# Bucket-masked attention and a routed expert layer: query tiles in groups of three in place of two

## The chip, the cores and the metric

The kernel runs on one NeuronCore of a Trainium2 chip. The metric is the device time of one execution in microseconds (us). The core has five engines that run side by side, each with its own queue: TensorE (PE; its weight loads are listed apart, as PEld), VectorE (DVE), ScalarE (ACT), GpSimd (POOL) and SyncE (SP), which here only issues DMA transfers. Semaphores order them against each other.

## What is computed

The inputs are q, k and v of shape (4, 8, 768, 64) in float32: 4 batches, 8 heads, 768 tokens, 64 numbers each. The attention is dense, with a mask from hashed buckets:

```python
q_bits = (np.einsum('bhsd,dk->bhsk', q, proj) > 0).astype(np.int64)
k_bits = (np.einsum('bhsd,dk->bhsk', k, proj) > 0).astype(np.int64)
...
mask = q_bucket[:, :, :, None] == k_bucket[:, :, None, :]
scores = scale * np.matmul(q, k.transpose(0, 1, 3, 2))
scores = np.where(mask, scores, -1000000000.0)
...
attn = attn / (np.sum(attn, axis=-1, keepdims=True) + 1e-09)
return np.matmul(attn, v).astype(np.float32)
```

The result, as 3072 tokens of 512 numbers, goes through an expert layer: each token is sent to the expert of its largest gate logit (one of 8), passes w1 (512 x 1024), a ReLU and w2 (1024 x 512) of that expert, and is scaled by two gates.

## The kernel before, in words

**Attention.** The 32 heads are worked off as 16 pairs (index g). A pair has 12 *steps*, so the attention has NSTEP = 192. One step is one tile of 128 queries of one head against all 768 keys. The first six steps of a pair (half hf = 0) cover the first 384 queries of its two heads, the last six the other 384. What happens to the tile of step s:

- `scores(s)`: four matmuls (L457; K = 128 and K = 76, each over two halves of the keys) into a PSUM tile `ps_s`, of which there are two. DVE then writes the masked scores to the SBUF tile `sc` and takes their minimum `mn` (L461). There are LAG + 2 tiles `sc`.
- `soft(s)`: ACT takes the exponential in place, and its row sum into one column of `rsum` (L469).
- `normal(s0)`: once for a group of steps. DVE adds 1e-9 to the group's row sums and takes the reciprocal (L476, L477); POOL multiplies each `sc` of the group by it (L479).
- `transposed(s)`: PE turns `sc` in six blocks of 128 x 128 (L490), three each into one of two PSUM tiles `ps_t`; ACT copies these to `pts` in SBUF, two copies of 128 x 384 (L491).
- `weighted(hb, c)`: a *pair of weighted sums*, one matmul for each of the two heads (L501): the values of key block c times `pts` of the half hb, added up in PSUM `ps_a` over c = 0 to 5. After the sixth pair DVE copies the sum to `ot` (L504).

**The order of the work.** PE, DVE, ACT and POOL run in the order in which the code is written; SP's transfers are placed by the framework's scheduler. The loop below writes the steps in groups of GROUP, here 2. In a group, each step writes its scores, then the transposition of the tile LAG steps back, then its exponential, then the small work that `plan` has put down for that step. At the start of a group `normal` handles the group before. At the end of a group come the pairs of weighted sums that the table `products` lists for its steps, one for each step.

```python
for s0 in range(0, NSTEP + LAG, GROUP):
    for s in range(s0, s0 + GROUP):
        if s < NSTEP:
            live[s] = scores(s)
        if s == s0 and 0 <= s - GROUP < NSTEP:
            normal(s - GROUP)
        if 0 <= s - LAG < NSTEP:
            transposed(s - LAG, live.pop(s - LAG))
        if s < NSTEP:
            live[s] = soft(s, *live[s])
        for fn in at.get(s, ()):
            fn()
    for s in range(s0, s0 + GROUP):
        for fn in products.get(s, ()):
            fn()
```

With GROUP = 2, LAG is 2 * GROUP = 4. `plan` places the preparation of the next pair of heads: `load` (queries and keys by DMA), `project` (bucket signs, L365), `split_hi` (POOL, L408) and `split_lo` (DVE, L416), which cut the operands into a high and a low part, `spread` (SBUF-to-SBUF DMAs that put the parts where the matmuls need them), and `load_v` (the pair's values `vt`, of which there are two buffers; L357). It also places `rows` (a DVE transpose, L513, and four DMAs to `x_dram`) and the routing of each finished batch (`logits`, L535, and others).

**Expert layer.** After the attention, the chosen expert's weights are streamed in and the tokens gathered; the change does not touch this part.

Of the kernel before, what the change touches and what calls it, by code (L numbers as in the profile page):

```python
# [19 lines left out]
B, H, S, D = 4, 8, 768, 64  # L20
# [19 lines left out]
TURN_DOWN = ((None, 0), (2, None), (None, 1), (3, None), (None, 2), (None, 3))  # L40
NROUND = (NTOK - min(CAPS) + CAP0 - 1) // CAP0
NCC = DM // P
GROUP = 2
NFB = F // P
MASKED = 1.0e9
PEN = float(2.0 ** 31)
# [10 lines left out]
def lsh_attention_then_moe(  # L57
# [26 lines left out]
    for h, s in ((0, 1.0), (1, -1.0)):  # L84
        hs = slice(h * D, (h + 1) * D)
        c = 2 * NB * h
# [239 lines left out]
    with ExitStack() as actx:  # L326
# [11 lines left out]
        at, products = {}, {}  # L338


        LAG = 2 * GROUP

        def plan(step, *fns):
            at.setdefault(step, []).extend(fns)


        def load(g, heads=(0, 1)):
            st = pairs[g]
            st.setdefault("qk", [])
            for j in heads:  # L350
                t = hp.tile([P, S], F32, name="qk", bufs=2)
                nc.sync.dma_start(t, qkT[2 * g + j])
                st["qk"].append(t)

        def load_v(g):
            pairs[g]["v"] = tp.tile([P, 2, NT, D], F32, name="vt", bufs=2)
            nc.sync.dma_start(pairs[g]["v"], v[g])  # L357

        def project(g, heads=(0, 1)):
            st = pairs[g]  # L360
            pp = ps_m.tile([P, HS], F32, name="ps_m")
            for j in heads:
                for n in range(2):
                    r = 32 * (2 * j + n)
                    nc.tensor.matmul(pp[r:r + 32], pjc[:, 0:32], st["qk"][j][:, n * HS:(n + 1) * HS],  # L365
                                     start=True, stop=True)
            bt = hp.tile([P, HS], F32R, name="bt", bufs=2)
            hs = slice(heads[0] * D, (heads[-1] + 1) * D)
            nc.vector.tensor_scalar(bt[hs], pp[hs], thr[hs], scl[hs], ALU.is_gt, ALU.mult)
            st["bt"] = bt  # L370
            for k in ("xl", "yl", "xr", "yr"):
                st.setdefault(k, [None, None])

        def first_head():

# [28 lines left out]

        def split_hi(g, j):
            st = pairs[g]
            xl = hp.tile([P, S], F32R, name="xl")
            nc.gpsimd.tensor_scalar(xl, st["qk"][j], sgn, 0.0, ALU.mult, ALU.add)  # L408
            st["xl"][j] = xl

        def split_lo(g, j, n):
            st = pairs[g]
            if n == 0:
                st["yl"][j] = hp.tile([P, S], F32R, name="yl")
            cs = slice(n * HS, (n + 1) * HS)
            nc.vector.scalar_tensor_tensor(st["yl"][j][:, cs], st["qk"][j][:, cs], sgn, f32(st["xl"][j][:, cs]),  # L416
                                           ALU.mult, ALU.subtract)

        def spread(g, j, hurry=False):
            st = pairs[g]  # L420
            xl, yl, bt = f32(st["xl"][j]), f32(st["yl"][j]), f32(st["bt"])
            st["xr"][j] = hp.tile([P, S], F32R, name="xr")
            st["yr"][j] = hp.tile([D + 2 * NB, S], F32R, name="yr")
            xr, yr = f32(st["xr"][j]), f32(st["yr"][j])
            if hurry:
                qk = st["qk"][j]
                for t in ("xr", "yr"):
                    nc.scalar.copy(st[t][j][0:D], qk[D:P])
                nc.gpsimd.tensor_scalar(st["xr"][j][D:P], yl[D:P], 1.0, 0.0, ALU.mult, ALU.add)
                nc.scalar.activation(st["xl"][j][D:P], qk[0:D], AF.Copy, scale=-0.125)  # L430
            else:
                nc.sync.dma_start(xr[0:D], xl[D:P])
                nc.sync.dma_start(yr[0:D], xl[D:P])
                nc.sync.dma_start(xr[D:P], yl[D:P])
                nc.sync.dma_start(xl[D:P], xl[0:D])
            for n in range(2):
                r = 32 * (2 * j + n)
                cs = slice(n * HS, (n + 1) * HS)
                nc.sync.dma_start(yr[D:D + 2 * NB, cs], bt[r + 2 * NB:r + 4 * NB])
                nc.sync.dma_start(yl[D:D + 2 * NB, cs], bt[r:r + 2 * NB])  # L440
# [8 lines left out]
        def scores(s):  # L449
# [5 lines left out]
            for l, r, k, first in ((st["xl"][j], st["xr"][j], P, True), (st["yl"][j], st["yr"][j], kb, False)):  # L455
                for n in range(2):
                    nc.tensor.matmul(ss[:, n, 0:HS], l[0:k, qs], r[0:k, n * HS:(n + 1) * HS],  # L457
                                     start=first, stop=not first)
            sc = tp.tile([P, 2, HS], F32, name="sc", bufs=LAG + 2)
            mn = sp.tile([P, 1], F32, name="mn")  # L460
# [3 lines left out]
        def soft(s, sc, mn):  # L464
            if s % GROUP == 0:
                sums[s // GROUP] = sp.tile([P, GROUP], F32, name="rsum")
            pr = sc.rearrange("p a b -> p (a b)")
            k = s % GROUP
            nc.scalar.activation(pr, pr, AF.Exp, bias=mn, scale=-1.0,  # L469
                                 accum_out=sums[s // GROUP][:, k:k + 1])  # L470
            return pr

        def normal(s0):

            rs = sums.pop(s0 // GROUP)
            nc.vector.tensor_scalar(rs, rs, 1e-9, None, ALU.add)  # L476
# [16 lines left out]
        def weighted(hb, c):  # L493
            g, hf = hb // 2, hb % 2
            st = pairs[g]
            if c == 0:
                st["av"] = ps_a.tile([P, HS], F32, name="ps_a")
            if c == NT - 1 and hf == 0:
                st["ot"] = gp.tile([P, S], F32, name="ot", bufs=4)
            for j in range(2):  # L500
                nc.tensor.matmul(st["av"][j * D:(j + 1) * D], st["v"][:, j, c], blocks[hb][j][:, c],  # L501
                                 start=(c == 0), stop=(c == NT - 1))
            if c == NT - 1:
                nc.vector.tensor_copy(st["ot"][:, hf * HS:(hf + 1) * HS], st["av"])  # L504

        def rows(g, hf, whole=True):

            b, i = divmod(g, H // 2)
            st = pairs[g]
            if hf == 0:  # L510
                st["xb"] = gp.tile([P, S // 32, 32], F32, name="xb", bufs=2)
            ts = slice(hf * HS // 32, (hf + 1) * HS // 32)
            nc.vector.transpose(st["xb"][:, ts].rearrange("p n c -> p (n c)"), st["ot"][:, hf * HS:(hf + 1) * HS])  # L513
            if whole:
                if hf == 0:
                    return
                ts = slice(0, S // 32)
            xv = x_dram[b * S:(b + 1) * S].rearrange("(n r) c -> r n c", r=32)
            for a in range(4):
                nc.sync.dma_start(xv[:, ts, i * P + 32 * a:i * P + 32 * (a + 1)], st["xb"][32 * a:32 * (a + 1), ts])  # L520
# [110 lines left out]
        for g in range(NP):  # L631
            s0 = 12 * (g - 1)
            if g >= 2:
                plan(s0 - 5, lambda g=g: load(g))
            if g >= 1:
                s0 += 2 * (g == 1)
                plan(s0 + 1, lambda g=g: project(g))
                plan(s0 + 5, lambda g=g: load_v(g))
                for j in range(2):
                    plan(s0 + 1 + 2 * j, lambda g=g, j=j: split_hi(g, j))  # L640
                    for n in range(2):
                        plan(s0 + 3 + 2 * j + n, lambda g=g, j=j, n=n: split_lo(g, j, n))
                    plan(s0 + 4 + 2 * j, lambda g=g, j=j: spread(g, j))
            for hf in range(2 if g + 1 < NP else 1):
                for c in range(NT):
                    products.setdefault(12 * g + 6 * hf + 6 + LAG + c, []).append(lambda hb=2 * g + hf, c=c: weighted(hb, c))
                if g + 1 < NP:
                    plan(12 * g + 6 * hf + 13 + LAG, lambda g=g, hf=hf: rows(g, hf))
        for b in range(B - 1):
            r = routing(b)  # L650
            for n, fn in ((11, lambda r=r: r["logits"](0, H // 2)), (12, lambda r=r: r["logits"](1, H // 2)),
                          (14, lambda r=r: r["tokens"](0, H // 2)), (16, lambda r=r: r["tokens"](1, H // 2)),
                          (18, r["best"]), (19, r["choose"]), (20, r["gates"]),
                          (22, r["prefix"]), (22, r["ranks"]), (23, r["cols"]), (24, r["hot"]), (26, r["table"]), (26, r["entries"])):
                plan(12 * (H // 2) * (b + 1) + n, fn)

        r = routing(B - 1)
        s0 = 12 * (NP - 1)
# [91 lines left out]
        with tc.manual_schedule(engines=MANUAL):  # L750
# [12 lines left out]
            live = {}  # L763
# [9 lines that stand above are left out]
# [58 lines left out]
    with tc.manual_schedule(engines=MANUAL):  # L831
# [16 lines left out]
        for r in range(E):  # L848
            n = CAPS[r] if r else CAP0
# [167 lines left out]
```

## Time and profile before

| what | value |
|---|---|
| median of 3 runs | 825.32 us (824.72 to 827.4) |
| profiled execution, its own time | 825.83 us |
| span of the profiled execution | 824.0 us |
| PE busy, share of the span | 779.8 us, 95% |
| DVE, ACT, POOL busy | 529.9, 460.9, 359.9 us |
| mean granted TensorE clock | 0.985 |

The span runs from the first to the last instruction of the program; the time of the execution is 1.8 us longer. In rows of the timeline the columns are start and duration in us, engine, line, operation, tiles, shapes and count; in square brackets stands how long the engine had been idle before, and what released it. PE's rows are pipelined, so starts of the weight loads (PEld) tell more of PE's pace than the lengths of its rows. A weighted-sum matmul and a transposition block have one or two records each: a pair of weighted sums shows as four records of L501, a transposition as six of L490.

### The profile page before, as it was taken

The page shows a single profiled execution, that of the slowest core. Times are in us where ns is not written, and L with a number is a line of the kernel's source. Part 1 is how long each engine was busy: PE and PEld are TensorE (multiplying, and loading weights), DVE is VectorE, ACT ScalarE, POOL GpSimd, SP SyncE. Part 2 cuts the span into 40 slices and gives each one's busy share as a digit, 9 for nine tenths or more (in the row PEclk, how much of TensorE's full clock was granted, in tenths as well). Part 3 has the DMA queues.
Part 4 walks back from the last instruction along what each step waited for, and adds up shares of the span by engine and source line. Part 5 has one row for each costly group of instructions (what it writes and reads, how often), then busy time and mean ns, then how long its engine had stood idle before and what let it go on. Part 6 is the DMA issues. An engine that isn't in the chain of part 4 may idle for free. (4 is left out here: it accounts for less than half of the span.)

```text
span 824.0 us, 13863 instructions
## 1 busy us (share of the span) xinstructions
PE 779.8 (95%) x4648; PEld 606.3 (74%) x4648; DVE 529.9 (64%) x1293; ACT 460.9 (56%) x934; POOL 359.9 (44%) x377
## 2 busy tenths in 40 slices
PE   6899999999999999999999998999999898979894
PEld 3667676677666666766767677888989897959693
DVE  5666666687656885765977562468586867575730
ACT  5767777677767777867777611442424242424240
POOL 5544445444544444544366843306171616160410
PEclk9999999999999999999999999999999999998998
DMA  3543654454455446445545323543545343535231
GB/s 120 135 101 90 140 123 90 117 136 103 108 132 133 82 113 149 92 106 135 132 104 143 85 71 116 179 133 113 169 131 168 131 155 121 160 121 170 89 101 36
DMA packets 84176, 99.54 MB, mean 121 GB/s; under 512 B 57183, under 2 KB 58671, under 8 KB 84096
## 3 DMA queue, kind: packets, MB, share of 16 engines
q1 hardware_dynamic: 79472, 84.66, 40.3%
q0 software_dynamic: 4480, 13.90, 4.9%
q8 instruction: 39, 0.64, 0.3%
q14 instruction: 41, 0.34, 0.1%
q10 hardware_dynamic: 144, 0.01, 0.0%
HBM read 60.07 MB, written 13.11 MB: 89 GB/s over the span
## 5 line engine op out<-in xcount | busy, mean ns | idle before, releaser
L479 POOL TENSOR_SCALAR sc<-sc,rsum 128x768 f32<-128x768 f32 x192 | 182.5, 963 | 224.6 <-DVE rsum L477 149.2
L461 DVE TENSOR_SCALAR_CACHE_REDUCE sc<-ps_s 128x768 f32<-128x768 f32 x192 | 183.2, 955 | 101.4 <-PE ps_s L457 95.6
L491 ACT COPY pts<-ps_t 128x384 f32<-128x384 f32 x384 | 164.3, 481 | 104.1 <-PE ps_t L490 103.6
L469 ACT ACTIVATE sc<-sc,mn 128x768 f32<-128x768 f32 x192 | 181.5, 945 | 12.7 <-DVE sc L461 11.5
L490 PE MATMUL ps_t<-ident,sc 128*128 128x128 f32 x1152 | 158.4, 273 | 1.5 <-POOL sc L479 0.7
L501 PE MATMUL ps_a<-pts,vt 128*64 128x384 f32 x768 | 145.9, 502 | 0.0
L490 PEld LDWEIGHTS ps_t<-ident,sc 128*128 128x128 f32 x1152 | 137.1, 140 | 11.6 <-POOL sc L479 3.0
L457 PE MATMUL ps_s<-xr,xl 128*128 128x384 f32 x384 | 117.9, 388 | 3.5 <-DMA xl<-xl 2.8
L270 PE MATMUL ps_s<-xh,w1h 128*128 128x256 f32 (+7 forms) x288 | 98.8, 343 | 8.7 <-POOL xh L254 4.9
L457 PEld LDWEIGHTS ps_s<-xr,xl 128*128 128x128 f32 x384 | 58.8, 193 | 63.3 <-issue 25.5
L270 PE MATMUL ps_s<-xlo,w1h 128*128 128x256 f32 (+7 forms) x288 | 96.9, 336 | 4.6 <-POOL xlo L255 4.3
L457 PE MATMUL ps_s<-yr,yl 76*128 76x384 f32 x384 | 100.7, 344 | 0.0
L270 PE MATMUL ps_s<-xh,w1l 128*128 128x256 f32 (+7 forms) x288 | 96.5, 335 | 1.6 <-DVE w1l L151 1.6
L250 DVE STREAM_TRANSPOSE xt<-xg 32x128 f32<-32x128 f32 x300 | 90.7, 302 | 5.7 <-POOL xlo L255 1.9
L287 POOL DMA_INDIRECT out_dram<-yo,sid x29 | 31.7, 1095 | 143.2 <-ACT yo L286 102.4
L501 PEld LDWEIGHTS ps_a<-pts,vt 128*64 128x64 f32 x768 | 46.9, 137 | 59.4 <-issue 54.5
L457 PEld LDWEIGHTS ps_s<-yr,yl 76*128 76x128 f32 x384 | 71.2, 192 | 0.2 <-DMA yl<-bt 0.2
L280 ACT ACTIVATE hh<-ps_s 128x256 fp32r<-128x256 f32 (+8 forms) x40 | 29.0, 726 | 70.2 <-PE ps_s L270 70.2
L281 DVE SCALAR_TENSOR_TENSOR hl<-ps_s,hh 128x256 fp32r<-128x256 f32 (+8 forms) x40 | 33.8, 848 | 50.2 <-ACT hh L280 49.6
L270 PEld LDWEIGHTS ps_s<-xh,w1h 128*128 128x128 f32 x288 | 55.0, 191 | 13.8 <-POOL xh L254 6.4
L150 ACT CAST w1h<-w_raw 128x1024 fp32r<-128x1024 f32 x28 | 28.8, 1046 | 64.5 <-DMA w_raw<-in_w_dram 64.4
L270 PEld LDWEIGHTS ps_s<-xlo,w1h 128*128 128x128 f32 x288 | 55.0, 191 | 7.3 <-POOL xlo L255 6.3
(185 smaller groups left out, 1061.8 us busy)
## 6 DMA issues: line engine op xcount, KB each, us to landing
w_raw<-in_w_dram SPq DMA_DIRECT2D x64, 512.0 KB
qk<-in_qkT_dram SPq DMA_DIRECT2D x32, 384.0 KB
vt<-in_v_dram SPq DMA_DIRECT2D x16, 384.0 KB
xr<-xl SPq DMA_DIRECT2D x30, 192.0 KB
yr<-xl SPq DMA_DIRECT2D x30, 192.0 KB
xr<-yl SPq DMA_DIRECT2D x30, 192.0 KB
xl<-xl SPq DMA_DIRECT2D x30, 192.0 KB
x_dram<-xb SPq DMA_DIRECT2D x60, 96.0 KB
```

The lines of the kernel that those rows point to most:

```text
L250: nc.vector.transpose(w[32 * a:32 * a + 32, :, q:q + 32], src[:, a])
L270: nc.tensor.matmul(ps, l, r, start=first and k == 0, stop=last and k == len(pairs) - 1)
L280: nc.scalar.activation(hh, ph, AF.Relu)
L281: return lambda: nc.vector.scalar_tensor_tensor(hl, ph, 0.0, f32(hh), ALU.max, ALU.subtract)
L287: nc.gpsimd.indirect_dma_start(out=out[:, :], out_offset=bass.IndirectOffsetOnAxis(ap=sid[0:n, r, a:a + 1], axis=0), in_=yo[0:n], in_offse ...
L457: nc.tensor.matmul(ss[:, n, 0:HS], l[0:k, qs], r[0:k, n * HS:(n + 1) * HS], start=first, stop=not first)
L461: nc.vector.tensor_scalar(sc, ss[:, :, 0:HS], MASKED, None, ALU.min, ALU.min, accum_out=mn)
L469: nc.scalar.activation(pr, pr, AF.Exp, bias=mn, scale=-1.0, accum_out=sums[s // GROUP][:, k:k + 1])
L479: nc.gpsimd.tensor_scalar(live[s0 + k], live[s0 + k], rs[:, k:k + 1], 0.0, ALU.mult, ALU.add)
L490: nc.tensor.transpose(tr[:, c], pr[:, (3 * h + c) * P:(3 * h + c + 1) * P], ident)
L491: nc.scalar.copy(pts[:, 3 * h:3 * h + 3, t * P:(t + 1) * P], tr)
L501: nc.tensor.matmul(st["av"][j * D:(j + 1) * D], st["v"][:, j, c], blocks[hb][j][:, c], start=(c == 0), stop=(c == NT - 1))
```

## The change

GROUP becomes 3, and LAG becomes GROUP + 1, which is 4 as before, so tiles and buffers keep their numbers. A group is now three steps, with three pairs of weighted sums at its end. The pairs of weighted sums are put down one step earlier (5 + LAG in place of 6 + LAG), `logits(0)` one step earlier (10 in place of 11), and `load_v` five steps later (10 in place of 5). Setting up the empty lists of a pair moves from `project` to `split_hi`, and does no work on the chip.

```diff
-GROUP = 2
+GROUP = 3
...
-        LAG = 2 * GROUP
+        LAG = GROUP + 1
...
-                plan(s0 + 5, lambda g=g: load_v(g))
+                plan(s0 + 10, lambda g=g: load_v(g))
...
-                    products.setdefault(12 * g + 6 * hf + 6 + LAG + c, []).append(lambda hb=2 * g + hf, c=c: weighted(hb, c))
+                    products.setdefault(12 * g + 6 * hf + 5 + LAG + c, []).append(lambda hb=2 * g + hf, c=c: weighted(hb, c))
...
-            for n, fn in ((11, lambda r=r: r["logits"](0, H // 2)), (12, lambda r=r: r["logits"](1, H // 2)),
+            for n, fn in ((10, lambda r=r: r["logits"](0, H // 2)), (12, lambda r=r: r["logits"](1, H // 2)),
```

**The order on PE, before,** in the group that starts at step 90. `ps_s` is the scores' tile, `sc` the tile that is transposed; the numbers tell tiles apart and have no relation between the two kernels. Four weighted sums follow.

```order
L457 MATMUL ps_s_2783<-xr_2402,xl_2308 128x384 x2
L457 MATMUL ps_s_2783<-yr_2403,yl_2365 128x384 x2
L490 MATMUL ps_t_2795<-ident_72,sc_2668 128x128 x3
L490 MATMUL ps_t_2800<-ident_72,sc_2668 128x128 x3
L457 MATMUL ps_s_2818<-xr_2467,xl_2367 128x384 x2
L457 MATMUL ps_s_2818<-yr_2468,yl_2435 128x384 x2
L490 MATMUL ps_t_2826<-ident_72,sc_2692 128x128 x3
L490 MATMUL ps_t_2831<-ident_72,sc_2692 128x128 x3
```

**The same place on PE with the change:** the group of steps 90, 91 and 92. Six weighted sums follow.

```order
L457 MATMUL ps_s_2737<-xr_2362,xl_2274 128x384 x2
L457 MATMUL ps_s_2737<-yr_2363,yl_2336 128x384 x2
L490 MATMUL ps_t_2750<-ident_72,sc_2624 128x128 x3
L490 MATMUL ps_t_2755<-ident_72,sc_2624 128x128 x3
L457 MATMUL ps_s_2773<-xr_2428,xl_2338 128x384 x2
L457 MATMUL ps_s_2773<-yr_2429,yl_2393 128x384 x2
L490 MATMUL ps_t_2781<-ident_72,sc_2651 128x128 x3
L490 MATMUL ps_t_2786<-ident_72,sc_2651 128x128 x3
L457 MATMUL ps_s_2796<-xr_2362,xl_2274 128x384 x2
L457 MATMUL ps_s_2796<-yr_2363,yl_2336 128x384 x2
L490 MATMUL ps_t_2804<-ident_72,sc_2680 128x128 x3
L490 MATMUL ps_t_2809<-ident_72,sc_2680 128x128 x3
```

A third step stands between two blocks of weighted sums; the tile transposed is that of four steps back in both.

**The multiplications on POOL and what they wait for on DVE, before.** POOL's rows, the tiles of steps 86 to 90:

```order
L479 TENSOR_SCALAR sc_2668<-sc_2668,rsum_2685 128x768
L479 TENSOR_SCALAR sc_2692<-sc_2692,rsum_2685 128x768
L479 TENSOR_SCALAR sc_2721<-sc_2721,rsum_2740 128x768
L479 TENSOR_SCALAR sc_2758<-sc_2758,rsum_2740 128x768
L479 TENSOR_SCALAR sc_2788<-sc_2788,rsum_2805 128x768
```

DVE's rows at step 90 (its minimum is the first row):

```order
L461 TENSOR_SCALAR sc_2788,mn_2789<-ps_s_2783 128x768
L476 TENSOR_SCALAR rsum_2740<-rsum_2740 128x2
L477 RECIPROCAL rsum_2740<-rsum_2740 128x2
L416 SCALAR_TENSOR_TENSOR yl_2776<-qk_2498,pj_64,xl_2708 128x384
L461 TENSOR_SCALAR sc_2823,mn_2824<-ps_s_2818 128x768
```

The tiles that PE transposes in this group, 2668 and 2692, are multiplied by `rsum_2685`, one group earlier than `rsum_2740`, whose reciprocal stands here.

**The same with the change.** POOL's rows, the tiles of steps 86 to 90:

```order
L479 TENSOR_SCALAR sc_2624<-sc_2624,rsum_2589 128x768
L408 TENSOR_SCALAR xl_2673<-qk_2459,pj_64 128x768
L479 TENSOR_SCALAR sc_2651<-sc_2651,rsum_2669 128x768
L479 TENSOR_SCALAR sc_2680<-sc_2680,rsum_2669 128x768
L479 TENSOR_SCALAR sc_2712<-sc_2712,rsum_2669 128x768
L479 TENSOR_SCALAR sc_2742<-sc_2742,rsum_2760 128x768
```

DVE's rows at step 90:

```order
L461 TENSOR_SCALAR sc_2742,mn_2743<-ps_s_2737 128x768
L476 TENSOR_SCALAR rsum_2669<-rsum_2669 128x3
L477 RECIPROCAL rsum_2669<-rsum_2669 128x3
L416 SCALAR_TENSOR_TENSOR yl_2728<-qk_2459,pj_64,xl_2673 128x384
L461 TENSOR_SCALAR sc_2778,mn_2779<-ps_s_2773 128x768
```

The tiles that PE transposes at the second and the third step of this group, 2651 and 2680, are now multiplied by `rsum_2669`, whose reciprocal stands in this same group, behind the minimum of its first step (`ps_s_2737`).

**The load of the values on SP,** before and then with the change:

```order
L434 DMA xr<-yl 64x768
L439 DMA yr<-bt 12x384
L357 DMA vt<-in_v_dram 128x768
L435 DMA xl<-xl 64x768
L440 DMA yl<-bt 12x384
```

```order
L440 DMA yl<-bt 12x384
L352 DMA qk<-in_qkT_dram 128x768 x2
L357 DMA vt<-in_v_dram 128x768
L520 DMA x_dram<-xb 32x24x32 x4
L432 DMA xr<-xl 64x768
```

It moves from the middle of a pair's spreading transfers to behind the loads of queries and keys.

More of the change, by code (lines that the diff above doesn't have):

```diff
@@ L370, in project @@
             st["bt"] = bt
-            for k in ("xl", "yl", "xr", "yr"):
-                st.setdefault(k, [None, None])
         def first_head():
@@ L406, in split_hi @@
             st = pairs[g]
+            for k in ("xl", "yl", "xr", "yr"):
+                st.setdefault(k, [None, None])
             xl = hp.tile([P, S], F32R, name="xl")
```

## The prediction

> **What bounds the kernel now.** First the page's busy times and groups, then the stages, then one group of steps row by row.
>
> ```profile
> PE 779.8 (95%) x4648; PEld 606.3 (74%) x4648; DVE 529.9 (64%) x1293; ACT 460.9 (56%) x934; POOL 359.9 (44%) x377
> ...
> L479 POOL TENSOR_SCALAR sc<-sc,rsum 128x768 f32<-128x768 f32 x192 | 182.5, 963 | 224.6 <-DVE rsum L477 149.2
> ...
> L490 PEld LDWEIGHTS ps_t<-ident,sc 128*128 128x128 f32 x1152 | 137.1, 140 | 11.6 <-POOL sc L479 3.0
> ```
>
> ```profile
> 10.00:33.70 23.70, 21.33 (x112) 15.52 (x112) 18.19 (x42) 18.86 (x42) 16.77 (x42) 1.00 0.48 126
> 33.70:44.90 11.20, 8.39 (x38) 4.76 (x36) 2.86 (x7) 4.32 (x10) 2.67 (x3) 0.70 0.36 78
> 44.90:460.90 416.00, 413.88 (x2710) 290.83 (x2708) 289.25 (x761) 311.00 (x718) 203.46 (x210) 1.00 0.50 116
> 460.90:473.20 12.30, 11.90 (x80) 7.15 (x78) 4.50 (x11) 8.39 (x19) 11.71 (x11) 1.00 0.49 115
> 473.20:824.00 350.80, 320.31 (x1705) 287.26 (x1703) 210.83 (x464) 112.92 (x141) 121.41 (x104) 0.97 0.41 127
> ```
>
> The columns are length, busy time of PE, PEld, DVE, ACT and POOL, the granted clock, and DMA. From 44.9 to 460.9 us the attention runs at full clock with PE idle for 2.1 us: PE's own pace is the bound, and POOL waits for others (224.6 us) while transpositions hardly ever wait for POOL (3.0 us). The expert layer, 350.8 us, is untouched. One plain group of the steady stage, without any planned matmul in it:
>
> ```profile
> 313.45 0.30 PEld L457 LDWEIGHTS ps_s<-xr,xl 128*128 128x128 f32 x2 [0.60 <-issue]
> ...
> 314.09 0.75 PEld L490 LDWEIGHTS ps_t<-ident,sc 128*128 128x128 f32 x6
> ...
> 314.55 0.96 DVE L461 TENSOR_SCALAR_CACHE_REDUCE sc<-ps_s 128x768 f32<-128x768 f32 x1 [1.81 <-PE ps_s L457]
> 314.79 0.86 ACT L491 COPY pts<-ps_t 128x384 f32<-128x384 f32 x2 [0.90 <-PE ps_t L490]
> 314.81 0.30 PEld L457 LDWEIGHTS ps_s<-xr,xl 128*128 128x128 f32 x2
> ...
> 315.44 0.16 DVE L476 TENSOR_SCALAR rsum<-rsum 128x2 f32<-128x2 f32 x1
> 315.45 0.75 PEld L490 LDWEIGHTS ps_t<-ident,sc 128*128 128x128 f32 x6
> 315.55 0.94 ACT L469 ACTIVATE sc<-sc,mn 128x768 f32<-128x768 f32 x1
> ...
> 315.63 0.17 DVE L477 RECIPROCAL rsum<-rsum 128x2 f32<-128x2 f32 x1
> ...
> 315.99 1.79 POOL L479 TENSOR_SCALAR sc<-sc,rsum 128x768 f32<-128x768 f32 x2 [2.47 <-DVE rsum L477]
> 316.37 0.20 PEld L501 LDWEIGHTS ps_a<-pts,vt 128*64 128x64 f32 x4 [0.17 <-issue]
> ...
> 317.81 0.30 PEld L457 LDWEIGHTS ps_s<-xr,xl 128*128 128x128 f32 x2 [0.60 <-issue]
> ```
>
> By weight loads: scores to transposition 0.64 (313.45 to 314.09), transposition to the next scores 0.72 (to 314.81), the last transposition to the weighted sums 0.92 (315.45 to 316.37), two pairs of sums 1.44 (to 317.81). A group takes 4.36 us, so three steps take 6.54.
>
> **What the larger group saves on PE.** The expert layer's start shows three pairs in one piece:
>
> ```profile
> 474.80 2.16 PE L501 MATMUL ps_a<-pts,vt 128*64 128x384 f32 x12
> 476.88 0.85 PE L555 MATMUL ps_m<-wgt,ot 128*128 128x32 f32 x6
> ```
>
> Three pairs take 2.08 us, so a pair costs 0.64 and each block 0.16 more. A group of three, if nothing waited: 3 x 0.64 + 2 x 0.72 + 0.92 + 2.08 = 6.36. That is 0.18 under 6.54; over 64 groups it would save 11.5 us.
>
> **The wait it adds.** In the new order, the tile that PE transposes at a group's second step is multiplied by POOL in that same group, behind the minimum of the group's first scores, the addition and the reciprocal. Before, that product stood a whole group earlier. The plain group gives the chain, counted from the first scores' weight load at 313.45: minimum +1.10, addition +1.99, reciprocal +2.18, POOL +2.54; two tiles take 1.79, so the first ends at about +3.44. Where a subtraction on DVE runs beside POOL, it ends a little later:
>
> ```profile
> 304.73 0.30 PEld L457 LDWEIGHTS ps_s<-xr,xl 128*128 128x128 f32 x2 [0.60 <-DVE yl L416]
> ...
> 306.90 0.60 DVE L416 SCALAR_TENSOR_TENSOR yl<-qk,pj,xl 128x384 fp32r<-128x384 f32 x1
> ...
> 307.18 1.98 POOL L479 TENSOR_SCALAR sc<-sc,rsum 128x768 f32<-128x768 f32 x2 [2.94 <-PE ps_s L457]
> ```
>
> Here POOL starts at +2.45, and with 0.90 for an undisturbed second tile the first ends at +3.53. How fast PE follows is seen after the last scores, where a transposition does wait:
>
> ```profile
> 465.40 1.78 POOL L479 TENSOR_SCALAR sc<-sc,rsum 128x768 f32<-128x768 f32 x2
> ...
> 466.35 0.64 PEld L490 LDWEIGHTS ps_t<-ident,sc 128*128 128x128 f32 x6 [0.69 <-POOL sc L479]
> ```
>
> The first tile ends near 466.30, and PE starts 0.05 later. So the second transposition can start at +3.49 to +3.58. PE reaches it at 1.36 + 0.64 = +2.00. The wait is 1.49 to 1.58 us; I take 1.54, the middle, since half of the groups have a subtraction there. Behind it stand the third scores, the third transposition and the sums. PE does not pass a waiting matmul, as one case shows, where the scores at 38.16 wait for a transfer:
>
> ```profile
> 31.59 1.79 POOL L479 TENSOR_SCALAR sc<-sc,rsum 128x768 f32<-128x768 f32 x2 [0.93 <-DVE rsum L477]
> ...
> 38.16 0.98 PE L457 MATMUL ps_s<-xr,xl 128*128 128x384 f32 x2 [2.81 <-DMA xl<-xl]
> ...
> 39.58 1.48 PE L490 MATMUL ps_t<-ident,sc 128*128 128x128 f32 x6
> 40.99 1.51 PE L365 MATMUL ps_m<-qk,pjc 128*32 128x384 f32 x8
> 42.43 2.56 PE L501 MATMUL ps_a<-pts,vt 128*64 128x384 f32 x8
> 44.92 0.44 PE L457 MATMUL ps_s<-xr,xl 128*128 128x384 f32 x1
> ```
>
> The transposition behind them had its tile from POOL by 33.4 and still ran at 39.58.
>
> Is something later still? The third transposition comes at 3.54 + 0.72 + 0.64 = +4.90; its tile is out of POOL at about +4.4. Its second PSUM half is asked for three loads later, +5.27, and ACT, which copies 0.70 after a transposition starts (314.09 to 314.79) and takes 0.86 for two copies, has freed it at 3.54 + 0.70 + 0.86 = +5.10. That holds with 0.17 to spare, so no second wait; lost by as much again, it would cost 0.2 a group, 12 us, the upper end of my range. ACT's exponential is done at +2.10 + 0.94, before the copies.
>
> So a group takes 6.36 + 1.54 = 7.90 us, 1.36 more than three steps before. From step 12 on there are 60 groups: **+81.6**.
>
> **Corrections.** Planned matmuls between the first transposition and the second scores are now hidden in the wait. These are `logits(1)` of three batches and two short pieces late:
>
> ```profile
> 448.13 0.85 PE L535 MATMUL ps_m<-ot,wgt 128*32 128x384 f32 x6
> 448.91 0.62 PE L457 MATMUL ps_s<-xr,xl 128*128 128x384 f32 x2
> ```
>
> 3 x 0.78 and about 0.7 for the two: **-3**. The first twelve steps are not paced by PE (21.3 of 23.7 us busy, at an unwarmed start): three groups there can lose 0 to 1.54 each; I take **+2.5**. In the stage of 33.7 to 44.9 the group of 11.2 us lost 6.1 to a late `xl` (2.81) and to the half clock after it. Steps 8 to 13 now last 1.54 + 0.64 longer, so most of that wait goes, with or without the half clock: -2.2 to -6.1, **-4**. After the last scores, six pairs and four transpositions remain as before: 0.
>
> **The load of the values** costs and gains nothing. It did wait for its buffer, with SP behind it:
>
> ```profile
> SPq L357 <- PE ps_a L501: 29.8, 13, 3.5
> ```
>
> But PE's 2.1 us of idle time in the steady stage bound all that a freer SP can give. At its new place it is issued some eleven steps before its first use.
>
> **Sum:** 81.6 - 3 + 2.5 - 4 = +77 on the profiled 825.8, so 903; the median of the runs stands 0.5 lower: **902 us**, 9% slower. Bounds: a chain 0.1 shorter takes off 8 with the start's best case; a third wait adds 12: 890 to 914.
>
> **Rivals.**
>
> A: *The wait does not occur*, because the reciprocal could be taken before the group's first minimum: DVE idles 1.81 us ahead of it. Then POOL would be ready before PE, and the time would be 825.3 - 11.5 = 814, faster. Against it: DVE's order puts the addition behind the minimum, and in every group quoted it ran there (315.44 after 314.55). Decided at +2.00: the multiplication would have to end 1.5 us earlier. Chance 4%.
>
> B: *The clock falls.* PE's idle time of about 1.3 us per 7.9 may drop the granted clock.
>
> ```profile
> 34.30:37.70 3.40, 1.05 (x9) 0.78 (x7) 1.21 (x4) 1.84 (x5) 1.44 (x2) 1.00 0.41 90
> 37.80:44.60 6.80, 6.44 (x26) 3.41 (x26) 1.64 (x3) 1.88 (x4) 1.13 (x2) 0.50 0.29 61
> ...
> 696.60:699.90 3.30, 1.78 (x9) 1.45 (x9) 0.11 (x1) 1.19 (x2) 1.98 (x2) 1.00 0.80 267
> 700.00:703.00 3.00, 2.36 (x13) 2.04 (x13) 1.02 (x1) 0.48 (x1) 0.00 (x0) 1.00 0.53 145
> ```
>
> A stretch of 3.4 us with PE 31% busy was followed by clock 0.50; one 54% busy was not. The new groups have at worst 2.1 of 3.4, 62%. Price: at half clock scores take 1.42 and a transposition 1.41 (38.16, 39.58, 40.99), two pairs 2.49 (42.43 to 44.92), three by ratio 3.6: a group takes 12.1, 4.2 more. One group in four, 15 of them, gives 902 + 63 = 965. Chance 5%. The Trainium skill, "TensorE: Matmul & The Clock Gate", section "A second HAM failure mode: psum-queue depth-cycling", speaks for this rival: short idle times of PE between groups of matmuls can make the clock swing between half and full. The trace has such idle times in the expert layer, with the clock at 1.00 behind the 54% stretch; by that section the estimate would be 965, by the row 902.
>
> C: *A second wait per group*: the third transposition also stands, for ACT's copies or a slower POOL, by 0.3 us: 902 + 18 = 920. The 0.17 us of room speaks against it. Chance 8%.
>
> D: *Half the wait is covered*, if POOL's chain proves 0.7 us shorter: 902 - 42 = 860. No row has it under 3.4. Chance 3%.
>
> **Chances.** Forecast (890 to 914) 80%, A 4, B 5, C 8, D 3. Range for 8 in 10, widened towards C: 888 to 920. A measurement of this kernel tells 0.3% from nothing: faster 4%, same 1%, slower 95%.
>
> **What would show it.** Right: PEld's transposition (L490) idle behind POOL's `sc` (L479) rises from 3.0 to about 90 us, some 60 times 1.5; plain groups last 7.9 us; PE's share falls to about 86%; SP's wait at L357 goes; the clock stays at 1.00 in the attention. Wrong: groups near 6.4 us (A), clock 0.5 in the steady stage (B), or L490 waiting for ACT `pts` as well (C).

## The result: 894.79 us, and the profile after

| | before | changed |
|---|---|---|
| median | 825.02 us (822.55 to 827.4, 4 runs) | 894.79 us (893.69 to 895.53, 4 runs) |
| ratio, 95% interval | | 1.0837 (1.0797 to 1.0876) |
| profiled execution, span | 824.0 us | 892.4 us, clock 0.989 |

The change makes the kernel 8.4% slower. The forecast was 902 us, with 888 to 920 as its range. The page of the changed kernel, busy times and one group:

```profile
PE 777.6 (87%) x4648; PEld 604.5 (68%) x4648; DVE 525.9 (59%) x1229; ACT 465.1 (52%) x934; POOL 359.7 (40%) x377
...
L490 PEld LDWEIGHTS ps_t<-ident,sc 128*128 128x128 f32 x1152 | 133.8, 141 | 103.3 <-POOL sc L479 97.3
```

Busy times are within some 4 us of those before; it is idle time that grew. Transpositions waited 3.0 us for POOL and now wait 97.3 us, about once in each of the 64 groups. A plain group of the changed kernel:

```profile
127.08 0.30 PEld L457 LDWEIGHTS ps_s<-xr,xl 128*128 128x128 f32 x2 [0.60 <-issue]
...
127.72 0.75 PEld L490 LDWEIGHTS ps_t<-ident,sc 128*128 128x128 f32 x6
128.18 0.96 DVE L461 TENSOR_SCALAR_CACHE_REDUCE sc<-ps_s 128x768 f32<-128x768 f32 x1 [0.42 <-PE ps_s L457]
129.26 0.18 DVE L477 RECIPROCAL rsum<-rsum 128x3 f32<-128x3 f32 x1
...
129.63 2.68 POOL L479 TENSOR_SCALAR sc<-sc,rsum 128x768 f32<-128x768 f32 x3 [5.08 <-DVE rsum L477]
130.59 0.64 PEld L490 LDWEIGHTS ps_t<-ident,sc 128*128 128x128 f32 x6 [1.50 <-POOL sc L479]
131.20 0.30 PEld L457 LDWEIGHTS ps_s<-xr,xl 128*128 128x128 f32 x2
...
131.84 0.75 PEld L490 LDWEIGHTS ps_t<-ident,sc 128*128 128x128 f32 x6
...
132.76 0.20 PEld L501 LDWEIGHTS ps_a<-pts,vt 128*64 128x64 f32 x4 [0.17 <-issue]
...
134.85 0.30 PEld L457 LDWEIGHTS ps_s<-xr,xl 128*128 128x128 f32 x2 [0.60 <-issue]
```

The chain stands as predicted: reciprocal at +2.18, POOL at +2.55, the second transposition at +3.51, where the predicted span was 3.49 to 3.58. The third transposition and the sums follow without a wait. This group takes 7.77 us. Of the 32 groups from step 12 on without planned matmuls, 31 take 7.76 to 8.00 us and average 7.88 (from the starts of their first weight loads); the other, that of step 174, takes 10.83 (see below).

Now both kernels cut at the same places: the first scores of step 0, of step 12 and of step 191, the expert layer's first matmuls, the end. The changed kernel:

```profile
9.90:37.80 27.90, 24.18 (x118) 17.93 (x116) 17.40 (x38) 19.94 (x43) 15.79 (x41) 1.00 0.46 119
37.80:534.70 496.90, 422.12 (x2758) 294.05 (x2756) 289.85 (x713) 320.55 (x730) 208.82 (x216) 1.00 0.41 99
...
544.40:892.40 348.00, 318.23 (x1706) 286.20 (x1704) 211.58 (x464) 113.72 (x143) 122.31 (x105) 0.98 0.41 128
```

The kernel before (its last stage is the 350.8 us shown with the prediction):

```profile
9.80:33.70 23.90, 21.53 (x114) 15.70 (x112) 18.24 (x42) 19.06 (x42) 16.98 (x42) 1.00 0.48 125
33.70:463.20 429.50, 424.57 (x2762) 297.10 (x2760) 293.82 (x773) 317.23 (x732) 208.35 (x216) 0.99 0.50 115
```

| stage | before | after | difference | predicted |
|---|---|---|---|---|
| first twelve steps | 23.89 | 27.95 | +4.1 | +2.5 |
| steps 12 to 191 | 429.53 | 496.89 | +67.4 | 81.6 - 3 - 4 = +74.6 |
| last scores to expert layer | 9.94 | 9.67 | -0.3 | 0 |
| expert layer | 350.83 | 347.96 | -2.9 | 0 |
| sum (spans) | 824.0 | 892.4 | +68.4 | +77 |

(From the starts of weight loads, to two digits; the first 9.8 us are the same within 0.05.) What the forecast missed lies in the second row, and that is what the experiments on the values were for.

### The profile page after: what moved, and what is told of

Its sections match the earlier page's. It is cut to its first block, busy times and chain, and to the rows that moved or that the text cites. A ratio compares the mean times of both kernels' runs of the same rounds, so it can differ in the third digit from the quotient of the medians.

```text
span 892.4 us, 13840 instructions
## 1 busy us (share of the span) xinstructions
PE 777.6 (87%) x4648; PEld 604.5 (68%) x4648; DVE 525.9 (59%) x1229; ACT 465.1 (52%) x934; POOL 359.7 (40%) x377
## 5 line engine op out<-in xcount | busy, mean ns | idle before, releaser
L490 PE MATMUL ps_t<-ident,sc 128*128 128x128 f32 x1152 | 162.7, 278 | 77.5 <-POOL sc L479 77.5
L490 PEld LDWEIGHTS ps_t<-ident,sc 128*128 128x128 f32 x1152 | 133.8, 141 | 103.3 <-POOL sc L479 97.3
L501 PE MATMUL ps_a<-pts,vt 128*64 128x384 f32 x768 | 138.0, 495 | 0.0
L501 PEld LDWEIGHTS ps_a<-pts,vt 128*64 128x64 f32 x768 | 49.3, 136 | 56.3 <-issue 55.8
```

Of the source, the lines that this page charges most:

```text
L490: nc.tensor.transpose(tr[:, c], pr[:, (3 * h + c) * P:(3 * h + c + 1) * P], ident)
```

## The experiments

The theory: a transposition waits for a product that POOL can only begin behind the group's first minimum, because with LAG short of two groups the tile belongs to the group just before. The rivals: three steps or three pairs of sums in a group cost something by themselves; or the values' new place does. Runs of one chip share the runs of the kernel before: for the first four experiments 824.75 us (818.19 to 829.02, 19 runs), for the last four 825.37 us (822.43 to 829.36, 11 runs).

### 1. The short distance alone, in groups of two

The kernel before with LAG less by one, and sums and `rows` kept at their places:

```diff
-        LAG = 2 * GROUP
+        LAG = 2 * GROUP - 1
...
-    products.setdefault(12 * g + 6 * hf + 6 + LAG + c, []) ...
+    products.setdefault(12 * g + 6 * hf + 7 + LAG + c, []) ...
...
-    plan(12 * g + 6 * hf + 13 + LAG, lambda g=g, hf=hf: rows(g, hf))
+    plan(12 * g + 6 * hf + 14 + LAG, lambda g=g, hf=hf: rows(g, hf))
```

> Groups of two as before, but LAG 3 in place of 4, so that the second tile that a group transposes is multiplied in that same group. Theory (the wait for a multiplication of the same group is the cost): a plain group of two goes from 4.36 to 4.36 + 1.54 = 5.90 us; over some 93 groups +143, less about 10 of planned matmuls that hide in the wait: 955 to 972 us. Rival (the group of three is the cost, by its longer blocks or by fuller PSUM buffers): the group is still two, so 823 to 830 us.

Measured: 936.38 us (one run), 111 us over the kernel before. A group of it:

```profile
170.51 0.30 PEld L457 LDWEIGHTS ps_s<-xr,xl 128*128 128x128 f32 x2 [0.60 <-issue]
...
174.02 0.64 PEld L490 LDWEIGHTS ps_t<-ident,sc 128*128 128x128 f32 x6 [1.50 <-POOL sc L479]
...
176.26 0.30 PEld L457 LDWEIGHTS ps_s<-xr,xl 128*128 128x128 f32 x2 [0.60 <-issue]
```

The same wait at the same place, +3.51, with no third step and the values where they were: the group takes 5.75 in place of 4.36, and the plain groups average 5.81. So the distance is enough to make the wait, and the size of the group is not needed for it. The total came below what was expected: 89 groups by 1.45 are 129, but steps 12 to 191 took only 104 more. The rest are things that cost time before and now lie under the wait: the late `xl` of step 12 (6), the projections' waits (8, see experiment 5) and planned matmuls (about 12).

### 2. The distance shorter by one more step, in groups of three

```diff
-        LAG = GROUP + 1
+        LAG = GROUP
...
-    products.setdefault(12 * g + 6 * hf + 5 + LAG + c, []) ...
+    products.setdefault(12 * g + 6 * hf + 6 + LAG + c, []) ...
...
-    plan(12 * g + 6 * hf + 13 + LAG, lambda g=g, hf=hf: rows(g, hf))
+    plan(12 * g + 6 * hf + 14 + LAG, lambda g=g, hf=hf: rows(g, hf))
```

> Groups of three, LAG 3 in place of 4: all three tiles that a group transposes are multiplied in that same group, the first included. Theory: PE comes to the first transposition 0.64 us into the group and its tile is out at 3.54, a wait of 2.90 in place of 1.54; the group goes from 7.90 to 9.26 us, +83 over 61 groups: 970 to 990 us. Rival (the group of three is the cost): as the changed kernel, 890 to 900 us.

Measured: 1084.85 us (one run), 95 over the upper end of the expectation. At full clock the group is close to it, 9.50 us, with the first transposition waiting:

```profile
102.75 0.30 PEld L457 LDWEIGHTS ps_s<-xr,xl 128*128 128x128 f32 x2 [0.60 <-issue]
...
106.45 0.64 PEld L490 LDWEIGHTS ps_t<-ident,sc 128*128 128x128 f32 x6 [3.05 <-POOL sc L479]
...
112.25 0.30 PEld L457 LDWEIGHTS ps_s<-xr,xl 128*128 128x128 f32 x2 [0.60 <-issue]
```

But only 4 of the 32 groups in steps 12 to 191 that carry no planned matmul ran so; the others took 10.6 to 12.3 us, for the granted clock kept falling. The columns of these rows are the prediction's (length, PE busy first, the clock behind POOL); the first row is steps 12 to 191, the others are stretches in it:

```profile
45.60:725.40 679.80, 521.43 (x2759) 381.81 (x2757) 281.79 (x713) 329.71 (x731) 207.12 (x218) 0.83 0.30 72
...
70.60:73.90 3.30, 0.67 (x8) 0.65 (x7) 1.73 (x5) 0.07 (x1) 1.79 (x2) 1.00 0.48 136
74.00:77.30 3.30, 3.30 (x15) 3.21 (x14) 0.96 (x2) 2.62 (x7) 0.97 (x2) 0.50 0.82 231
...
104.70:108.00 3.30, 1.54 (x12) 1.51 (x13) 0.89 (x5) 0.91 (x3) 2.70 (x3) 1.00 0.00 0
108.10:111.40 3.30, 3.29 (x24) 2.23 (x24) 3.30 (x7) 3.30 (x9) 0.94 (x2) 1.00 0.35 74
111.50:114.80 3.30, 1.72 (x10) 0.79 (x6) 1.51 (x5) 0.72 (x2) 0.10 (x1) 1.00 0.63 161
114.90:121.70 6.80, 5.86 (x24) 5.67 (x25) 1.43 (x4) 3.76 (x8) 2.65 (x3) 0.50 0.68 181
```

This is the prediction's rival B, in another kernel: waits of 2.85 to 3.4 us, one in each group, bring it, where 1.50 us does not. In the expert layer of this same run the clock is 0.98, as in the changed kernel, so the fall belongs to the attention and not to the run as a whole.

### 3. The distance longer by one step, in groups of three

```diff
-        LAG = GROUP + 1
+        LAG = GROUP + 2
...
-            sc = tp.tile([P, 2, HS], F32, name="sc", bufs=LAG + 2)
+            sc = tp.tile([P, 2, HS], F32, name="sc", bufs=LAG + 1)
...
-    products.setdefault(12 * g + 6 * hf + 5 + LAG + c, []) ...
+    products.setdefault(12 * g + 6 * hf + 4 + LAG + c, []) ...
...
-    plan(12 * g + 6 * hf + 13 + LAG, lambda g=g, hf=hf: rows(g, hf))
+    plan(12 * g + 6 * hf + 12 + LAG, lambda g=g, hf=hf: rows(g, hf))
```

> Groups of three, LAG 5 in place of 4 (six score tiles, as before): the first two tiles that a group transposes come from the group before, and only the third is of the same group. Theory: PE comes to the third at 3.36 us and its tile is out at 3.54, so 0.1 to 0.2 us are left of the wait; ACT's copies may add 0.1 to 0.2. A group takes 6.5 to 6.7 us, and the time is 812 to 830 us, near the kernel before. Rival (the group of three is the cost): above 880 us.

Measured: 822.15 us (816.07 to 825.61, 10 runs), ratio 0.9969 (0.9935 to 1.0003). Here a group's first two transpositions take tiles of the group before last, and only the third takes one of the group's fresh products. One step more of distance takes off 72.6 us, the whole of the 69.8 that the change cost: three steps in a group and three pairs of sums at its end are not what is slow. 28 of the 32 plain groups average 6.57, between the 6.36 without any wait and 7.88; three (steps 66, 114 and 162) take 7.39, and that of step 174 takes 10.84.

### 4. The sums of the group before taken ahead of the first scores

The changed kernel with LAG 4 kept, and only `normal` written earlier, so that DVE has the addition and the reciprocal ahead of the group's first minimum:

```diff
         for s in range(s0, s0 + GROUP):
+            if s == s0 and 0 <= s - GROUP < NSTEP:
+                normal(s - GROUP)
             if s < NSTEP:
                 live[s] = scores(s)
-            if s == s0 and 0 <= s - GROUP < NSTEP:
-                normal(s - GROUP)
```

> As the changed kernel (groups of three, LAG 4), but the addition and the reciprocal of the row sums stand ahead of the minimum of the group's first scores on DVE, not behind it. Theory (the chain from the first scores over the minimum to the multiplication sets the wait): the chain now starts at the end of the last exponential of the group before, 0 to 1 us into the group, so the first tile is out at 1.4 to 2.4 us against 2.00 when PE comes; a group takes 6.4 to 6.9 us and the time is 815 to 845 us. Rival (POOL's three multiplications in a row, not the place of the reciprocal, make the wait): above 870 us.

Measured: 819.48 us (817.37 to 824.88, 10 runs), ratio 0.9932 (0.9904 to 0.996).

```profile
112.73 0.30 PEld L457 LDWEIGHTS ps_s<-xr,xl 128*128 128x128 f32 x2 [0.60 <-issue]
...
113.51 0.18 DVE L477 RECIPROCAL rsum<-rsum 128x3 f32<-128x3 f32 x1
...
113.83 0.96 DVE L461 TENSOR_SCALAR_CACHE_REDUCE sc<-ps_s 128x768 f32<-128x768 f32 x1
113.88 2.70 POOL L479 TENSOR_SCALAR sc<-sc,rsum 128x768 f32<-128x768 f32 x3 [3.95 <-PE ps_s L457]
...
116.34 0.64 PEld L490 LDWEIGHTS ps_t<-ident,sc 128*128 128x128 f32 x6 [0.23 <-issue]
...
119.23 0.19 PEld L457 LDWEIGHTS ps_s<-xr,xl 128*128 128x128 f32 x1 [0.60 <-issue]
```

The reciprocal stands at +0.78 in place of +2.18, POOL starts at +1.15 in place of +2.55, and the wait of 1.50 is gone. A group takes 6.50. With the distance, the group size and the tables of the changed kernel kept, 75 us go by the order on DVE alone. That settles the cause: it is the way from the minimum over the reciprocal to POOL. (The 0.23 us left ahead of the third transposition have no releaser in the trace; the copies on ACT end there, but that is an inference.)

### 5. The later load of the values alone, in groups of two

The kernel before with only this line changed:

```diff
-                plan(s0 + 5, lambda g=g: load_v(g))
+                plan(s0 + 10, lambda g=g: load_v(g))
```

> The kernel before (groups of two), with the load of the values five steps later, as in the change, and nothing else. Theory A (the later load frees SP, and the loads of queries and keys behind it land before the bucket projection asks for them): of the 8.7 us that the projections' weight loads waited for queries and keys, some 5 go: 817 to 821 us. Theory B (as the prediction had it, the load's place costs and gains nothing): 823 to 827 us.

Measured: 813.91 us (812.8 to 817.02, 6 runs), ratio 0.9859 (0.9828 to 0.9891): 11.5 us faster, more than either theory had. Where from: SP in the kernel before (issue of transfers), and what PE did with the queries and keys that come last there:

```profile
226.09 0.60 SPq L434 DMA_DIRECT2D xr<-yl  x1
230.21 0.36 SPq L357 DMA_DIRECT2D vt<-in_v_dram  x1
...
234.43 0.98 SPq L352 DMA_DIRECT2D qk<-in_qkT_dram  x2
```

```profile
237.97 0.84 PE L365 MATMUL ps_m<-qk,pjc 128*32 128x384 f32 x4 [0.52 <-DMA qk<-in_qkT_dram]
239.13 0.84 PE L365 MATMUL ps_m<-qk,pjc 128*32 128x384 f32 x4 [0.32 <-DMA qk<-in_qkT_dram]
```

The same place with the values loaded later (their load stands behind these), SP and then PE:

```profile
222.64 0.59 SPq L434 DMA_DIRECT2D xr<-yl  x1
...
228.65 0.98 SPq L352 DMA_DIRECT2D qk<-in_qkT_dram  x2
```

```profile
233.81 0.87 PE L365 MATMUL ps_m<-qk,pjc 128*32 128x384 f32 x8
```

The load of the values stood 3.5 us (226.69 to 230.21) at the head of SP's queue for its buffer, and the transfers behind it came later, the next queries and keys last: 8.3 us after the transfer out of `yl`, and 6.0 us with the values moved. The projection then waited on PE. It is four matmuls, two for each head, which show as eight rows. With the values moved, the rows of the two heads run side by side, and all eight are done in 0.87 us. Before, the second head's four rows start 1.16 us behind the first's, and each four take 0.84 by themselves. What L365 took (ns: shortest, median, longest) and what PE and PEld together waited for ahead of it, in the kernel before and in this experiment, the start of the kernel included:

```profile
L365 PE MATMUL ps_m<-qk,pjc x124: 486/510/849, 8.4 to 411.9; 128*32 128x384 f32 x124
...
  DMA qk<-in_qkT_dram: 11.4, 17
```

```profile
L365 PE MATMUL ps_m<-qk,pjc x124: 486/510/849, 8.5 to 402.6; 128*32 128x384 f32 x124
...
  DMA qk<-in_qkT_dram: 2.5, 2
```

So no row got shorter. The time in which any of them ran did: in the 13 groups with a projection behind step 12 it is 16.6 us before and 11.1 here, and PE's idle time ahead of these rows is 2.1 us before and none here. PE's idle time was no bound, because part of PE's *busy* time was there only since the two heads' data came apart.

Group by group: 14 groups of steps 12 to 191 hold a projection. Here ten of them take 5.14 to 5.16 us, and three with other planned matmuls 6.12; before, 13 of the 14 (all but step 12's) took 7.8 us more in sum. Step 12's own group, with the half clock, became 1.7 shorter, and no plain group changed (4.36). Together that is, within 0.1, the 9.4 us which steps 12 to 191 lost; the expert layer gave 2 more, which lies within the spread given further below.

### 6. The early load, in groups of three

The changed kernel with that line put back to `s0 + 5`.

> The changed kernel with the load of the values at its old place (five steps after a pair's start). Theory A (the place matters by itself, here too): the projections wait again for queries and keys, 3 to 7 us more than the changed kernel's 894.8: 898 to 902 us. Theory B (nothing, or the longer steps of this kernel hide it): 893 to 897 us.

Measured: 896.34 us (893.9 to 898.91, 6 runs), ratio 1.0859 (1.0825 to 1.0894), the same as the changed kernel within the intervals. The load waits less for its buffer there:

```profile
SPq L357 <- PE ps_a L501: 10.3, 12, 2.1
```

(29.8 us before, and no such row in the changed kernel.) The rows of L365 waited 2.2 us in all for queries and keys there and 2.4 in the changed kernel, against 11.4 in the kernel before. A pair of heads now takes 5 us longer, and it seems that this gives SP the time that it lacked. The later load brings 11.5 us where PE sets the pace, and nothing where POOL's products do.

### 7. and 8. What is left in a group of three

To see what a group of three is worth once nothing waits, experiment 7 adds to experiment 3 that a step's exponential is written behind the next step's transposition, so that ACT copies first:

```diff
-            if s < NSTEP:
-                live[s] = soft(s, *live[s])
+            if s > s0 and s - 1 < NSTEP:
+                live[s - 1] = soft(s - 1, *live[s - 1])
             for fn in at.get(s, ()):
                 fn()
+        if s < NSTEP:
+            live[s] = soft(s, *live[s])
         for s in range(s0, s0 + GROUP):
```

> Groups of three, LAG 5, and ACT's exponential of a step stands behind the copies of the next step's transposition (the last of a group at its end), so that copies no longer queue behind an exponential. Theory (without the wait for POOL, ACT's copies set 0.13 us of a plain group's 6.49): the group falls towards 6.36 us, 61 groups x 0.1: 5 to 8 us under LAG 5 alone, 812 to 818 us, unless the 0.1 us left of the wait for POOL takes its place (then 820 to 824). Rival (PE's switch between tile shapes costs more than the rows of before gave): 6.49 stays, 820 to 824 us, and PE waits for nothing that the profile shows.

Measured: 817.76 us (816.03 to 821.7, 7 runs), ratio 0.9919 (0.989 to 0.9948). The same 28 plain groups as in experiment 3 average 6.53 (6.40 to 6.70); in a group of 6.50 the third transposition still waits 0.23 us for POOL. Experiment 8 adds experiment 4's order of `normal`:

> As the run with LAG 5 and the later exponential, with the addition and the reciprocal also ahead of the group's first minimum. Theory (two waits bound the group of three, for POOL's product and for ACT's copies, and now neither is left): a plain group takes 6.36 to 6.40 us, 809 to 816 us, faster than every kernel so far. Rival (the last exponential of a group, now later, holds the reciprocal and with it the minimum and the scores): a group stays at 6.5 us or more, 819 us or above.

Measured: 810.37 us (808.66 to 813.93, 6 runs), ratio 0.9814 (0.9781 to 0.9847), the lowest median of all versions.

```profile
109.23 0.30 PEld L457 LDWEIGHTS ps_s<-xr,xl 128*128 128x128 f32 x2 [0.60 <-issue]
...
115.59 0.30 PEld L457 LDWEIGHTS ps_s<-xr,xl 128*128 128x128 f32 x2 [0.60 <-issue]
```

A plain group takes 6.36 us, just what the prediction worked out for three steps without a wait. Against experiment 5 that should be worth 0.18 in each of some 60 groups, 11 us; steps 12 to 191 are only 2.9 shorter (417.2 against 420.1). Of the 8 us between, 4.8 went to the group of step 174, where the expert layer's first gathers stand ahead of POOL's products (see below), 2.9 to the 14 groups with a projection, which cost 0.99 over a plain group in place of 0.78, and 3.5 to four more: in those of steps 66, 114 and 162 PE still waits 0.8 us for POOL, and in that of step 48 the projection waits for queries and keys again. Step 12's group gives some 2.5 back. Why a projection costs more here was not tried.

## Why the prediction was right, and where it was off

**The wait: right, by its own mechanism.** The second transposition starts at +3.51 (predicted 3.49 to 3.58), a plain group takes 7.88 (7.90), PEld waits 97.3 us behind POOL (about 90), and PE's share is 87% (86%). Experiments 1 and 4 show the cause from both sides. The wait is a little longer beside DVE's work, where groups take 7.96 to 8.00, and a restarted PE runs the next loads a little closer (0.61 from the transposition to the scores in place of 0.72), so the mean comes out level.

**The third wait (rival C) did not come.** The 0.17 us of room held. **Rival A** (no wait) is false in the changed kernel, but experiment 4 is this rival made true: 819.5, where the prediction had 814.

**Rival B (the clock) came once in place of 15 times.** A stretch with one of the ordinary waits of the changed kernel in it, and the stretch behind it:

```profile
112.40:115.80 3.40, 1.99 (x16) 1.67 (x15) 3.37 (x8) 1.98 (x5) 2.01 (x3) 1.00 0.00 0
115.80:119.20 3.40, 3.40 (x23) 1.91 (x21) 2.37 (x5) 3.28 (x8) 2.08 (x3) 1.00 0.53 132
```

PE was busy for 59% of it, and the clock stayed at 1.00, as in all of steps 12 to 191 but for one place: behind the one wait of 3.0 us, in the group of step 174, it was at 0.50 for some 3.4 us. The other 59 waits for POOL in these steps, of 0.5 to 2.0 us, left it at 1.00.

```profile
491.34 1.14 PEld L490 LDWEIGHTS ps_t<-ident,sc 128*128 128x128 f32 x6 [3.01 <-POOL sc L479]
```

```profile
491.00:491.90 0.90, 0.56 (x3) 0.56 (x4) 0.00 (x0) 0.00 (x0) 0.90 (x2) 0.66 0.63 138
491.90:494.40 2.50, 2.50 (x12) 2.40 (x11) 0.20 (x1) 1.88 (x4) 1.14 (x2) 0.50 0.99 273
```

The Trainium skill ("TensorE: Matmul & The Clock Gate", "A second HAM failure mode: psum-queue depth-cycling") tells of a kernel in which short idle times of PE between groups of matmuls make the clock swing. In this case's traces waits of 1.5 us did not; a wait of 3 us did, once here and all along in experiment 2.

The length of a wait does not settle it alone. Three waits of 2.02 us in the changed kernel left the clock at 1.00, while in experiments 3, 7 and 8 it fell to 0.50 in the group of step 174, where the longest waits are 2.12, 2.17 and 1.92 us.

**The step that failed** is "The load of the values costs and gains nothing", with its reason, "PE's 2.1 us of idle time in the steady stage bound all that a freer SP can give." Experiment 5 measured 11.5 us for that load alone in groups of two. The reason took PE's busy time for a fixed amount of work. It was not: the projections of 13 groups kept PE busy for 16.6 us where 11.1 do, since the second head's rows ran behind the first's and not beside them. With the 2.1 us of idle time, all of it ahead of these rows, that makes 7.6 of the 7.8 us that these groups lost. The waits of L365 in the kernel before (11.4 us, PE and PEld together) show it; PE's idle time alone does not.

In the changed kernel the gain does not come from the load's new place (experiment 6); the longer groups alone take these waits away. Either way the prediction had left them in.

**The terms of steps 12 to 191,** from the starts of the weight loads, groups counted to step 189:

| term | predicted | measured |
|---|---|---|
| longer groups | +81.6 (60 x 1.36) | +79.1 (59 x 7.88 - 88.5 x 4.36) |
| planned matmuls hidden | -3 | -2.6 |
| late `xl` at step 12 and half clock | -4 (-2.2 to -6.1) | -6.1 (11.19 to an ordinary group) |
| projections' waits | 0 | -7.8 |
| group of step 174 | 0 | +2.9 (10.83 - 7.88) |
| projections dearer (0.87 for 0.78), last two steps | 0 | +1.8 |
| sum (67.4 in the stages; the terms are rounded) | +74.6 | +67.3 |

The group of step 174 shows that the change put POOL on the path. POOL's rows there:

```profile
487.89 1.18 POOL L226 DMA_INDIRECT xg<-x_dram,gid  x1 [3.20 <-DVE gid L692]
489.38 0.96 POOL L226 DMA_INDIRECT xg<-x_dram,gid  x1 [0.31 <-DVE yl L416]
490.36 0.93 POOL L479 TENSOR_SCALAR sc<-sc,rsum 128x768 f32<-128x768 f32 x1
```

Two gathers for the expert layer are issued ahead of the products; these start at +4.03 in place of about +2.5 (the group starts at 486.33), the transposition waits 3.01, and the half clock shown above follows. In the kernel before, the groups of steps 174 and 176 take 4.36 and 4.43.

**First twelve steps:** +4.1 for +2.5; the bound was three groups by 0 to 1.54 (4.6), and the true value lies near its upper end. **Expert layer:** -2.9 was not predicted. In the ten profiled executions of all kernels, the time from the last weighted sums to the end lies between 341.3 and 346.5 us, 345.0 before and 342.1 after, so this difference says nothing of the change.

So 902 was 7 us too high: -7.8 for the projections' waits and -2.9 in the expert layer make up more than all of it. The other misses (-2.5 in the longer groups, -2.1 at step 12, +2.9 at step 174, +1.8 for dearer projections and the last two steps, +1.6 in the first twelve) nearly cancel, and that is luck. One sum of the prediction is off as well: 902 less 8 is 894, not the 890 that it takes as its lower bound; the measured time lies just inside both.

## What to carry to other kernels

When a group of steps grows, count the distance from producer to consumer in groups, not in steps: four steps back is two whole groups of two, but only one and a third of three, and the consumer then waits for a chain that starts in its own group. The cheapest cure is often to write the small link of that chain (here an addition and a reciprocal of 128x3) ahead of the large operation that it queues behind. And do not take an engine's idle time as the bound on what a freer transfer queue can give: work that could run side by side may be standing one behind the other because its data come apart, and then it counts as busy. The waits of the weight loads show it.

## What the runs showed of the hardware that was not expected

- The rows of two heads' projection matmuls ran side by side on TensorE: eight rows of 0.49 to 0.51 us were done in 0.87 us, and four of them alone took 0.84. When the second head's data came late, the same rows stood as 0.84 twice. PE then showed 0.52 and 0.32 us of idle time, where the weight loads showed 0.76 and 1.02.
- The granted clock fell to 0.50 behind waits of 2.8 us (the late `xl` of the kernel before) and 3.0 us (the group of step 174 after), and in that group of experiments 3, 7 and 8, whose longest waits are 1.9 to 2.2 us. It did not fall behind 59 waits of 0.5 to 2.0 us in the changed kernel. By stretches of some 3.4 us, it fell behind such with PE 20% and 52% busy (experiment 2) and 31% (kernel before), and not behind such with 47% (experiment 2), 54% (kernel before) and 59% (changed kernel). So neither the wait nor the busy share of one stretch alone decides it near these values; where the stretches begin may matter, and no run here shows that.
- One load for each pair of heads that waits up to 3.5 us at the head of SP's queue delayed what stood behind it. Issuing it five steps later made the kernel before 11.5 us faster; the profiles show 9.4 us of that in steps 12 to 191.
